# A fused attention, gated-MLP and gated-convolution kernel: its opening issued in another order

## The chip, the cores and the metric

The kernel runs on one core of one Trainium2 chip. The metric is the device time of one execution in microseconds (us). The profile's span, from the first to the last recorded instruction, is a little shorter than that time. The core has five engines that matter here, each with its own in-order instruction queue: TensorE (PE; its weight loads are listed as PEld), VectorE (DVE), ScalarE (ACT), GpSimd (POOL) and SyncE (SP), which here only issues DMA transfers. Semaphores tie the queues together.

## The reference

Three layers in sequence, in float32, on 8 batches of 576 tokens and 512 channels:

```python
scores = scale * q @ k.T                        # per batch and head (8 heads of 64)
x = (scores * Dmat) @ v                         # Dmat: gamma_h ** (i - j) for i >= j, else 0

h = gelu_tanh(x @ w_in)                         # 512 -> 1024
u, v = h[..., :512], h[..., 512:]
v_n = (v - mean(v)) / sqrt(var(v) + 1e-6) * g_ln
v_s = einsum('ts,bsd->btd', w_sg, v_n) + b_sg   # mix over the 576 tokens
x = x + (u * v_s) @ w_out

gate = sigmoid(causal 5-tap convolution of x)
out = (gate * (x @ w_val)) @ w_out2
```

The weights `w_in`, `w_out`, `w_val`, `w_out2` and `conv_w` arrive as float64.

## The kernel before

**Attention** is done in 24 groups (8 batches, three groups of 192 tokens each), and a group in three chunks of 64 tokens. For group i, `load_kq(i)` and `load_v(i)` fetch its keys (384 KB), its queries in three layouts (960 KB) and its values (576 KB) on SP's queue into rings of two buffers. Then come `k_decay` (ACT, four products a chunk), `scores` (PE, 24 products into the PSUM tile `sc`), `masked` (DVE, `sc` times the decay mask into `pt`), `adds` (PE, keys times values into `st`), `states` (DVE, running sums of `st`, a step a chunk), `state_decay` (DVE), `q_decay` (DVE), `outputs` (PE, into `xo`), `out_copy` (ACT, `xo` to `xg`), `out_high` (ACT, the rounded part of x, and the store of x to DRAM on ACT's DMA queue) and `out_low` (DVE, the rest of x). `sc`, `st`, `xo` and `pt` have one buffer each, `sums` and `qp` two. The last group of a batch has two chunks in `adds` and `states`, the first has a smaller `q_decay`. A float32 product of PE leaves two MATMUL and two LDWEIGHTS records in the trace: `scores` 48 of each, `adds` 48 or 32, `outputs` 96, or 80 in the first group of a batch.

**`w_in`** is fetched in four blocks g of 256 columns (1 MB each) into `raw_in`, which has two halves (g % 2), and decoded from float64 bits into a high and a low part, `wi`. `decode` returns ten steps: steps 0 and 9 run on ACT, steps 1, 2, 3, 5 and 7 are DVE tensor_scalar operations, 4, 6 and 8 are DVE scalar_tensor_tensor operations. `d[0]` and `d[1]` are the two parts of block 0, and `d[2]`, `d[3]`, `d[4]` are blocks 1 to 3. All blocks share one set of temporaries, `tmp_in`.

**The MLP's first product** is cut into `u_tile(b, n)` (12 matmuls of 288 columns, blocks 0 and 1 of `w_in`; even n needs tokens 0 to 287, odd n the rest) and `v_tile(b, s)` (12 matmuls of 512 columns, blocks 2 and 3, 128 tokens each; tile 4 of an odd batch holds the last 64 tokens of two batches). `u_gelu`, `v_gelu`, `v_norm` and `v_high` follow on ACT, `v_stat` on DVE and POOL, and `v_low` on DVE. PSUM has two buffers for these tiles. `mix` is the product over tokens; it needs `w_sg` (split by `split_w_sg` on DVE after `fetch_w_sg`, through two `raw` buffers) and all `v` tiles of its batch. The split `w_sg` lies in the buffer that holds x of batch 0, so that `split_w_sg(0)` waits for the last product on that x.

**The order.** From line 721 on, the order of the opening is written out by hand, one call a line, and it is the order within each engine's queue: 49 warm-up products on zeros, `w_in`, the attention groups 0 to 5 and part of 6, and all 16 `u` tiles of batches 0 and 1. From line 926 a planner sorts the rest by due times: the nine `v` tiles of batches 0 and 1 (list `slow`), then `outputs(6)`, the first mix and everything after it.

Of the kernel before, what the change touches and what calls it, by code (L numbers as in the profile page):

```python
# [23 lines left out]
GC = 3  # L24
# [113 lines left out]
def fused_kernel(  # L138
# [50 lines left out]
    with ExitStack() as p1:  # L189
# [268 lines left out]

        def states(i):

            if i >= NGR:
                return
            t = grp[i]
            if i % NG == 0:
                t["sums"] = sts.tile([128, GC, 2, 2 * D], F32, tag="sums", name="sums")
            for j in range(chunks(i)):
                new = t["st"][:, :, 2 * D * j : 2 * D * (j + 1)]
                if j < GC - 1:
                    to = t["sums"][:, j + 1]
# [37 lines left out]

        def out_copy(i):
# [18 lines left out]
        def out_high(i):  # L527
# [17 lines left out]
            act.dma_start(out=x1d[:, i], in_=xc)  # L545
# [83 lines left out]
        def u_tile(b, n):  # L629
            m, h = n // 2, n % 2  # L630
            if n == 0:
                bt[b]["u"] = upool.tile([128, KT, S], F32, tag="u", name="u")
# [101 lines left out]
        sync.dma_start(out=dm_sb, in_=dmask)  # L734
        fetch_w_in(0, 1, 4)
        sync.dma_start(out=kf_sb, in_=kfac)
        load_kq(0)
        load_kq(1)
        d[0][0]()
        sync.dma_start(out=qf_sb, in_=qfac)  # L740
        d[0][1]()
        load_v(1)
        d[0][2]()
        fetch_w_in(1)
        d[0][3]()
        d[0][4]()
        d[0][9]()
        d[0][5]()
        d[0][6]()
        d[0][7]()  # L750
        d[0][8]()
        d[1][0]()
        d[1][1]()
        d[1][2]()
        d[1][3]()
        d[1][4]()
        scores(0, False)
        k_decay(0, act, (0,))
        d[1][5]()
        masked(0)  # L760
        k_decay(0, act, (2,))
        d[1][6]()
        k_decay(0, act, (1,))
        d[1][7]()
        d[1][9]()
        adds(0)
        d[1][8]()
        scores(1, False)
        k_decay(1, act, (1,))
        states(0)  # L770
        k_decay(1, act, (2,))
        k_decay(1, act, (0,))
        q_decay(0)
        state_decay(1)
        outputs(0)
        load_kq(2)
        q_decay(1)
        adds(1)
        out_copy(0)
        masked(1)  # L780
        load_v(2)
        out_high(0)
        states(1)
        load_kq(3)
        d[2][0]()
        d[2][1]()
        outputs(1)
        d[2][2]()
        out_low(0)
        out_copy(1)  # L790
        scores(2, False)
        q_decay(2)
        k_decay(2, act, (1,))
        state_decay(2)
        k_decay(2, act, (0,))
        masked(2)
        out_high(1)
        adds(2)
        d[2][3]()
        load_kq(4)  # L800
        states(2)
        load_v(3)
        out_low(1)
        outputs(2)
        d[2][4]()
        k_decay(3, act, (1,))
        scores(3, False)
        d[2][5]()
        k_decay(3, act, (0,))
        load_v(4)  # L810
        fetch_w_in(2)
        u_tile(0, 0)
        masked(3)
        k_decay(3, act, (2,))
        d[2][6]()
        d[2][9]()
        u_tile(0, 2)
        d[2][7]()
        u_gelu(0, 0)
        d[2][8]()  # L820
        scores(4, False)
        k_decay(4, act, (1,))
        q_decay(4)
        u_tile(0, 4)
        k_decay(4, act, (2,))
        q_decay(3)
        u_gelu(0, 2)
        adds(3)
        out_copy(2)
        u_tile(0, 6)  # L830
        k_decay(4, act, (0,))
        states(3)
        load_kq(5)
        u_gelu(0, 4)
        out_high(2)
        state_decay(4)
        outputs(3)
        u_gelu(0, 6)
        out_low(2)
# [3 lines left out]
        states(4)  # L843
        u_tile(0, 1)
        d[3][0]()
        out_high(3)
        d[3][1]()
        u_tile(0, 5)
        u_gelu(0, 1)
        d[3][2]()  # L850
        out_low(3)
        k_decay(5, act, (0,))
        masked(4)
        u_tile(0, 3)
        u_gelu(0, 5)
        k_decay(5, act, (1,))
        state_decay(5)
        q_decay(5)
        outputs(4)
        u_gelu(0, 3)  # L860
        d[3][3]()
        d[3][4]()
        scores(5, False)
        load_v(6)
        fetch_w_in(3)
        out_copy(4)
        adds(5)
        masked(5)
        out_high(4)
        u_tile(0, 7)  # L870
        d[3][9]()
        out_low(4)
        states(5)
        u_tile(1, 0)
        u_gelu(0, 7)
        d[3][5]()
        d[3][6]()
        outputs(5)
        u_gelu(1, 0)
        d[3][7]()  # L880
        u_tile(1, 2)
        out_copy(5)
        load_v(7)
        d[3][8]()
        load_kq(6)
        out_high(5)
        u_tile(1, 6)
        u_gelu(1, 2)
        out_low(5)
        d[4][0]()  # L890
        u_tile(1, 4)
        u_gelu(1, 6)
        d[4][1]()
        d[4][2]()
        u_tile(1, 1)
        u_gelu(1, 4)
        d[4][3]()
        d[4][4]()
        u_tile(1, 7)
        u_gelu(1, 1)  # L900
        d[4][5]()
        k_decay(6, act, (2,))
        q_decay(6)
        u_tile(1, 5)
        u_gelu(1, 7)
        d[4][6]()
        k_decay(6, act, (0,))
        u_tile(1, 3)
        k_decay(6, act, (1,))
        d[4][7]()  # L910
        d[4][8]()
        u_gelu(1, 5)
        scores(6, False)
        u_gelu(1, 3)
        d[4][9]()
        adds(6)
        masked(6)
        load_kq(8)
        states(6)
        load_kq(7)  # L920
        state_decay(7)
# [3 lines left out]


# [104 lines left out]
        slow = [("v", 0, s) for s in range(4)] + [("v", 1, s) for s in (4, 0, 1, 2, 3)]  # L1031
# [17 lines left out]
        at(0.0, fetch_w_sg, 0)  # L1049
        at(0.0, fetch_w_sg, 1)  # L1050
# [452 lines left out]
```

## Time and profile before

| | us |
|---|---|
| median of 3 executions | 717.16 (717.13 to 718.82) |
| the profiled execution | 717.23 |
| its span | 715.4 |
| PE busy in the span | 692.2 (97%) |
| DVE busy | 567.8 (79%) |
| ACT busy | 387.2 (54%) |
| POOL busy | 137.1 (19%) |

The profiled execution took 1.83 us more than its span, and it lies 0.07 us from the median. PE is idle for 23.2 us of the span. The page cuts the span into 40 slices of 17.9 us; PE's busy tenths there are 3 in the first slice, 7 in the second and in the last, and 9 in the 37 others. So a reader looks at the opening first. A row of the timeline gives start, duration, engine, line, operation, output and inputs and a count. In the chain of work that ended last, a row gives start, length and what the chain passed through; "issue" is time for which the profile shows no releaser.

### The profile page before, as it was taken

To read this page: it belongs to the slowest core of one execution; us is meant where nothing else is said; L and a number is where in the kernel's file an instruction comes from. 1 tells how busy PE (TensorE), PEld (TensorE's weight loads), DVE (VectorE), ACT (ScalarE), POOL (GpSimd) and SP (SyncE) were. 2 spreads that over 40 slices of the span, in tenths; PEclk is the share of its full clock that TensorE was granted. 3 is DMA by queue.
4 is the path that set the end of the run, shared out by engine and by line. 5 is a ranking of instruction groups with operands and counts; after the bars stand their busy time and mean duration, and the time that the engine had idled before them with its cause. 6 is when DMAs were issued, how large, how long until landed. Compare 5 with 4: busy or idle time off the path is not lost.

```text
span 715.4 us, 20119 instructions
## 1 busy us (share of the span) xinstructions
PE 692.2 (97%) x8658; PEld 661.4 (92%) x8658; DVE 567.8 (79%) x899; ACT 387.2 (54%) x692; POOL 137.1 (19%) x210
## 2 busy tenths in 40 slices
PE   3799999999999999999999999999999999999997
PEld 3689889899998998998998999999999999999997
DVE  5677788797697786886865657989899998989893
ACT  5656583562744635536426134676566665656542
POOL 0000340410410302303004002222223231212100
PEclk9689999999999999999999999999999999999999
DMA  9978439699489989498872899899679896745404
GB/s 338 350 273 275 180 105 310 200 289 368 111 242 343 278 252 327 87 304 322 210 226 41 297 393 244 278 223 191 167 166 206 192 213 159 175 118 75 109 1 150
DMA packets 69578, 157.15 MB, mean 220 GB/s; under 512 B 5873, under 2 KB 43889, under 8 KB 67697
## 3 DMA queue, kind: packets, MB, share of 16 engines
q1 hardware_dynamic: 35440, 97.90, 38.9%
q0 software_dynamic: 22016, 39.23, 29.0%
q10 hardware_dynamic: 12032, 18.73, 7.1%
q8 instruction: 68, 1.11, 0.6%
q14 instruction: 22, 0.17, 0.1%
HBM read 109.54 MB, written 54.26 MB: 229 GB/s over the span
## 4 chain that ended last, share of the span: by engine, by line
PE 87%; DVE 5%; DMA 5%; ACT 1%; issue 1%; SPq 1%; DVEq 0%; ACTq 0%
PE ps L1158 24%; PE ps_u L183 14%; PE ps L1277 14%; PE ps_v L568 14%; PE ps_m L655 10%; PE sc L424 3%; DMA raw_g<-g1d 3%; PE xo L502 2%; PE xo L494 2%; DMA qk_sb<-in_qk 2%; PE st L440 2%; PE ps_m L663 2%; DVE op L165 1%; DVE xl L165 1%; ACT op L162 0%
## 5 line engine op out<-in xcount | busy, mean ns | idle before, releaser
L655 PE MATMUL ps_m<-ws,vh 128*128 128x288 f32 x768 | 114.0, 297 | 0.7 <-DVE gt L672 0.7
L655 PEld LDWEIGHTS ps_m<-ws,vh 128*128 128x128 f32 x768 | 104.8, 188 | 2.5 <-DVE gt L672 1.4
L1277 PE MATMUL ps<-op,wv 128*128 128x288 f32 x768 | 102.7, 294 | 0.0
L1277 PEld LDWEIGHTS ps<-op,wv 128*128 128x128 f32 x768 | 101.9, 188 | 0.0
L1158 PE MATMUL ps<-op,wo 128*128 128x288 f32 x672 | 92.2, 297 | 1.1 <-DVE op L165 1.0
L1158 PEld LDWEIGHTS ps<-op,wo 128*128 128x128 f32 x672 | 90.7, 188 | 1.8 <-DVE op L165 1.2
L183 PE MATMUL ps_u<-xh,wi 128*128 128x288 f32 x448 | 91.7, 296 | 0.0
L1158 PE MATMUL ps<-op,wf 128*128 128x288 f32 x672 | 90.8, 296 | 0.0
L1158 PEld LDWEIGHTS ps<-op,wf 128*128 128x128 f32 x672 | 90.1, 188 | 0.0
L1250 DVE SCALAR_TENSOR_TENSOR gate<-x,cw_sb,gate 128x576 f32<-128x576 f32 x114 | 87.5, 812 | 1.0 <-ACT gate L1232 1.0
L183 PEld LDWEIGHTS ps_u<-xh,wi 128*128 128x128 f32 x448 | 72.6, 188 | 0.6
L568 PE MATMUL ps_v<-wi,xh 128*128 128x512 f32 x224 | 70.8, 397 | 0.0
L183 PE MATMUL ps_u<-xl,wi 128*128 128x288 f32 x224 | 66.0, 295 | 0.0
L162 ACT CAST op<-raw_g 128x1152 fp32r<-128x1152 f32 (+1 forms) x36 | 36.7, 1036 | 46.1 <-PE ps L1277 20.5
L514 ACT COPY xg<-xo 128x768 f32<-128x768 f32 x24 | 19.1, 797 | 66.6 <-PE xo L502 60.9
L595 POOL TENSOR_SCALAR rs<-mv 128x1 f32<-128x1 f32 x36 | 10.1, 280 | 229.9 <-DVE mv L594 218.5
L1168 ACT COPY s<-ps 128x576 f32<-128x576 f32 x48 | 30.8, 641 | 37.9 <-PE ps L1158 35.5
L585 ACT ACTIVATE vt<-ps_v 128x512 f32<-128x512 f32 x36 | 21.5, 597 | 53.8 <-PE ps_v L568 53.3
L568 PEld LDWEIGHTS ps_v<-wi,xh 128*128 128x128 f32 x224 | 41.4, 188 | 9.9 <-DVE gt L672 0.2
L672 DVE SCALAR_TENSOR_TENSOR gt<-ps_m,g_sb,b_sb 128x288 f32<-128x288 f32 x64 | 32.8, 515 | 20.9 <-PE ps_m L663 20.8
L1210 POOL DMA_DIRECT2D x<-x1d x24 | 31.3, 1542 | 84.1 <-DVE x L1199 83.2
L165 DVE TENSOR_TENSOR op<-raw_g,op 128x1152 fp32r<-128x1152 f32 (+1 forms) x36 | 42.9, 1202 | 5.5 <-ACT op L162 5.5
(124 smaller groups left out, 1298.3 us busy)
## 6 DMA issues: line engine op xcount, KB each, us to landing
qk_sb<-in_qk SPq DMA_DIRECT2D x24, 960.0 KB, 8.2
raw_g<-g1d SPq DMA_DIRECT2D x8, 2016.0 KB, 8.4
vv_sb<-in_vv SPq DMA_DIRECT2D x24, 576.0 KB, 5.5
g1d<-g1d POOLq DMA_DIRECT2D x48, 288.0 KB, 5.8
g1d<-u SPq DMA_DIRECT2D x40, 288.0 KB, 7.4
kk_sb<-in_kk SPq DMA_DIRECT2D x24, 384.0 KB, 6.0
x1d<-xg ACTq DMA_DIRECT2D x24, 384.0 KB, 6.0
x<-x1d POOLq DMA_DIRECT2D x24, 384.0 KB, 6.8
```

What stands on the lines that cost most here:

```text
L162: return act.copy(dst, src) if engine is act else engine.tensor_copy(dst, src)
L165: return dve.tensor_tensor(dst, src, high.bitcast(F32), op=ALU.subtract)
L183: pe.matmul(ps[:, :n], lhs, rhs[:, k, x_cols], start=i == 0, stop=i == last)
L568: pe.matmul(ps, lhs, rhs, start=i == 0, stop=i == KT * 3 - 1)
L585: act.activation(vt, vs[b, s][0], AF.Gelu_apprx_tanh)
L655: pe.matmul(ps[:, :n], lhs, rhs, start=first, stop=False)
L672: dve.scalar_tensor_tensor(gt, mx.pop((b, i))[:, :n], g_sb[:, m : m + 1], b_sb[:, t0 : t0 + n], op0=ALU.mult, op1=ALU.add)
L1158: pe.matmul(got(ps)[:, o, :HN], lhs, rhs, start=first and i == 0, stop=last and i == 5, skip_group_check=True,)
L1168: add("ACT", act_us(2 * HN), lambda: act.copy(got(key), full(ps)), (ps,), (key,), stage=stage)
L1210: lambda g=g, at=at: pool.dma_start(out=L["x2"][par][:, :, at : at + GT], in_=x1d[:, i * NG + g], accum_op=ALU.add), mine, [("x2", par, "g ...
L1250: lambda gt=gt, x2=x2, m=m, j=j: dve.scalar_tensor_tensor(gt(), x2(j), cw_sb[:, m, j : j + 1], gt(), op0=ALU.mult, op1=ALU.add), (*x2_keys ...
L1277: pe.matmul(ps[:, mm, :HN], lhs, rhs, start=j == 0, stop=j == 3 * KT - 1, skip_group_check=True)
```

## The change

The calls of the opening stand in another order, and more of them stand in it. The nine `v` tiles with all their steps, `q_decay(7)`, `k_decay(7)`, and the fetches and splits of `w_sg` move from the planner's list into the order by hand (`slow` is now empty, and `load_conv` has a due time 25.1 less, as nine tiles of 2.79 are gone from ahead of it). Four helpers are cut finer: `load_kq` into `load_k` and `load_q`, `states` into `state_step`, and the store of x (`out_store`) out of `out_high`. Block 0 of `w_in` is cut into halves (1:1) where it was 1:3. The warm-up products stay. No arithmetic is added or taken away. The first loads, and the middle of the new order:

```diff
-        d = [decode_w_in(0, 0, 1), decode_w_in(0, 1, 4)] + [decode_w_in(g) for g in range(1, 4)]
-        fetch_w_in(0, 0, 1)
+        d = [decode_w_in(0, 0, 2), decode_w_in(0, 2, 4), decode_w_in(1), decode_w_in(2), decode_w_in(3)]
+        fetch_w_sg(1)
+        sync.dma_start(out=dm_sb, in_=dmask)
+        fetch_w_sg(0)
+        load_v(0)
+        load_k(0)
+        sync.dma_start(out=kf_sb, in_=kfac)
+        load_q(0)
+        fetch_w_in(0, 2, 4)
         sync.dma_start(out=gf_sb, in_=gfac)
-        load_v(0)
...
+        load_v(1)
+        load_k(1)
         sync.dma_start(out=qf_sb, in_=qfac)
+        fetch_w_in(0, 0, 2)
+        load_q(1)
         fetch_w_in(1)
...
-        slow = [("v", 0, s) for s in range(4)] + [("v", 1, s) for s in (4, 0, 1, 2, 3)]
+        slow = []
...
-        load_conv(34.0)
+        load_conv(8.9)
```

The order of each queue after the change, up to the first mix (groups and tiles by number; ss is a `state_step`, sd `state_decay`, qd `q_decay`):

```
PE   warm x49, scores 0, adds 0, outputs 0, adds 1, scores 1, adds 2, outputs 1, scores 2, outputs 2,
     u(0,2) u(0,6), scores 3, u(0,4), adds 3, scores 4, u(0,0) u(0,5) u(0,7) u(0,1) u(0,3), outputs 3,
     adds 4, v(0,0) v(0,1), adds 5, scores 5, outputs 4, v(0,2) v(0,3), outputs 5, u(1,4) u(1,0), adds 6,
     u(1,2) u(1,3), v(1,4) v(1,0) v(1,1) v(1,2) v(1,3), u(1,7) u(1,5) u(1,1), scores 6, u(1,6), outputs 6, mix
DVE  d1.3 d1.5, masked 0, d1.6, ss 0.0, d1.1, ss 0.1, d1.2, qd 0, ss 0.2, d1.4 d0.3 d1.7 d0.5 d1.8 d0.1,
     sd 1, d0.2, ss 1.0, qd 1, out_low 0, d0.4 d0.6 d0.7, ss 1.1, d0.8, ss 1.2, d2.3, sd 2, masked 1, qd 2,
     d2.1, ss 2.0, d2.2, ss 2.1, d2.4 d2.5 d2.7, masked 2, d2.6, out_low 1, d3.1 d2.8 d3.2 d3.5 d3.3 d3.6 d3.4,
     masked 3, d3.7, out_low 2, d3.8 d4.1, ss 3.0, d4.5 d4.3 d4.6 d4.2, qd 3, d4.4, ss 3.1, d4.7, ss 3.2, d4.8, ...
SP   w_sg 1, dmask, w_sg 0, v 0, k 0, kfac, q 0, w_in 0 (half), gfac, v 1, k 1, qfac, w_in 0 (half), q 1,
     w_in 1, k 2, q 2, v 2, k 3, w_in 2, q 3, k 4, v 3, q 4, w_in 3, v 4, k 5, q 5, v 5, k 6, q 6, ...
```

In the kernel before, PE ran all 16 `u` tiles before the first `v` tile, and the first `u` tile stood after `scores(3)`.

## Rows read from the trace of the kernel before

**Rows 1.** Windows: length; busy us (records) of each engine; PEclk; DMA share; GB/s.

```profile
10.00:20.00 10.00, 5.67 (x211) 5.27 (x215) 8.68 (x14) 6.10 (x24) 0.00 (x0) 0.95 1.01 414
20.00:30.00 10.00, 6.93 (x256) 6.42 (x250) 6.32 (x10) 6.71 (x16) 0.00 (x0) 0.67 0.94 339
30.00:40.00 10.00, 8.40 (x164) 7.72 (x157) 7.69 (x11) 5.09 (x14) 0.00 (x0) 0.53 0.96 358
```

**Rows 2.** The chain that ended last, of 0 to 160: start, length, what.

```profile
26.52 1.91 issue
...
36.41 4.75 PE ps_u L183 x24
41.16 0.86 PE sc L424 x48
...
54.64 0.28 PE xo L494 x8
...
62.30 11.35 PE ps_u L183 x84
...
75.22 25.34 PE ps_v L568 x108
100.57 0.39 PE xo L502 x16
...
101.89 1.78 PE ps_m L655 x12
```

**Rows 3.** DVE by line and shape, 0 to 110: busy, mean ns of one, idle.

```profile
L474 DVE TENSOR_TENSOR sums<-st,sums 128x256 f32<-128x256 f32 x19 | 8.0, 423 | 3.0 <-PE st L440 2.5
L452 DVE TENSOR_TENSOR pt<-sc,dm_sb 128x768 f32<-128x768 f32 x8 | 7.6, 955 | 6.2 <-PE sc L424 5.4 <-PE xo L502 0.8
L236 DVE SCALAR_TENSOR_TENSOR wi<-tmp_in 128x1024 fp32r<-128x1024 f32 x3 | 3.7, 1225 | 0.1
L235 DVE TENSOR_SCALAR tmp_in<-tmp_in 128x1024 uint32<-128x1024 uint32 x3 | 2.1, 687 | 0.0
L236 DVE SCALAR_TENSOR_TENSOR wi<-tmp_in 128x768 fp32r<-128x768 f32 x1 | 1.0, 959 | 0.0
```

**Rows 4.** DVE timeline: two neighbours on other data, then two on the same.

```profile
51.15 0.95 DVE L165 TENSOR_TENSOR xl<-xg,xh 128x768 fp32r<-128x768 f32 x1
52.02 0.95 DVE L452 TENSOR_TENSOR pt<-sc,dm_sb 128x768 f32<-128x768 f32 x1
...
61.49 0.69 DVE L235 TENSOR_SCALAR tmp_in<-tmp_in 128x1024 uint32<-128x1024 uint32 x1
62.21 1.23 DVE L236 SCALAR_TENSOR_TENSOR wi<-tmp_in 128x1024 fp32r<-128x1024 f32 x1
```

**Rows 5.** SP timeline: issue of q 0 and of w_in 2.

```profile
4.25 0.63 SPq L380 DMA_DIRECT2D qk_sb<-in_qk  x1
...
35.56 0.42 SPq L253 DMA_DIRECT2D raw_in<-in_w_in  x1
```

**Rows 6.** DMA issues alone: q 0, w_in 2, w_in 1: KB, us to landing.

```profile
qk_sb<-in_qk SPq DMA_DIRECT2D x1, 960.0 KB, 7.5
...
raw_in<-in_w_in SPq DMA_DIRECT2D x1, 1024.0 KB, 7.4
...
raw_in<-in_w_in SPq DMA_DIRECT2D x1, 1024.0 KB, 12.7
```

**Rows 7.** PE timeline: the part of scores 1 ahead of PE's first halt.

```profile
15.25 0.78 PE L424 MATMUL sc<-qk_sb 64*64 64x64 f32 x28 [0.48 <-DMA qk_sb<-in_qk]
```

**Rows 8.** PE alone, from the end of one halt to the next (clock, DMA).

```profile
22.40:28.42 6.02, 3.90 (x127) 0.72 0.94 326
28.42:33.79 5.37, 3.77 (x127) 0.57 0.94 341
```

**Rows 9.** Windows of 2 us around the first u tiles, columns as in rows 1.

```profile
36.00:38.00 2.00, 2.00 (x22) 1.88 (x17) 1.53 (x2) 0.01 (x1) 0.00 (x0) 0.50 0.94 330
...
40.00:42.00 2.00, 2.00 (x58) 1.77 (x56) 1.89 (x3) 2.00 (x10) 0.00 (x0) 1.00 0.62 254
```

More of the change, by code (lines that the diff above doesn't have):

```diff
@@ L764, in fused_kernel @@
+        state_step(0, 0)
+        k_decay(1, act, (0,))
+        d[1][1]()
+        state_step(0, 1)
+        d[1][2]()
+        k_decay(1, act, (2,))
+        q_decay(0)
+        state_step(0, 2)
+        outputs(0)
+        load_q(2)
+        k_decay(1, act, (1,))
+        d[1][4]()
+        d[0][3]()
+        d[1][9]()
         d[1][7]()
-        d[1][9]()
-        adds(0)
+        d[0][5]()
+        d[0][0]()
         d[1][8]()
-        scores(1, False)
-        k_decay(1, act, (1,))
-        states(0)
@@ L771, in fused_kernel @@
[L771 to L777, printed above, removed]
         adds(1)
         out_copy(0)
-        masked(1)
[L781 to L785, printed above, removed]
+        load_v(2)
+        d[0][1]()
+        state_decay(1)
+        load_k(3)
+        scores(1, False)
+        out_store(0)
+        out_high(0, False)
+        d[0][2]()
+        state_step(1, 0)
@@ L786, in fused_kernel @@
+        q_decay(1)
+        out_low(0)
+        d[0][4]()
+        d[0][6]()
+        d[0][9]()
+        d[0][7]()
+        k_decay(2, act, (0,))
+        fetch_w_in(2)
+        state_step(1, 1)
+        d[0][8]()
+        d[2][0]()
+        state_step(1, 2)
+        d[2][3]()
+        k_decay(2, act, (1,))
+        load_q(3)
+        state_decay(2)
+        masked(1)
+        q_decay(2)
+        adds(2)
         d[2][1]()
         outputs(1)
+        k_decay(3, act, (1,))
+        load_k(4)
+        state_step(2, 0)
@@ L811, in fused_kernel @@
[L811 to L821, printed above, removed]
-        k_decay(4, act, (1,))
[L823 to L828, printed above, removed]
+        k_decay(3, act, (0,))
+        state_step(2, 1)
+        d[2][4]()
+        k_decay(3, act, (2,))
@@ L842, in fused_kernel @@
         load_v(5)
[L843 to L850, printed above, removed]
-        out_low(3)
[L852 to L856, printed above, removed]
-        state_decay(5)
[L858 to L862, printed above, removed]
-        scores(5, False)
[L864 to L921, printed above, removed]
+        masked(4)
+        v_tile(0, 0)
+        load_k(6)
+        out_high(3, False)
+        state_step(4, 0)
+        q_decay(4)
+        out_store(3)
+        out_low(3)
+        load_q(6)
+        state_step(4, 1)
+        v_tile(0, 1)
+        q_decay(5)
+        v_gelu(0, 0)
+        state_step(4, 2)
+        v_stat(0, 0)
+        state_decay(5)
+        k_decay(6, act, (0,))
+        adds(5)
+        v_gelu(0, 1)
+        scores(5, False)
+        state_step(5, 0)
         sync.dma_start(out=b_sb, in_=b_sg)
@@ L924, in fused_kernel @@
         sync.dma_start(out=conv_raw.rearrange("p n t -> p (n t)"), in_=conv_w)
+        load_k(7)
+        k_decay(6, act, (2,))
+        v_stat(0, 1)
+        outputs(4)
+        load_q(7)
+        state_step(5, 1)
+        k_decay(6, act, (1,))
+        v_tile(0, 2)
+        masked(5)
+        load_v(6)
+        v_norm(0, 0)
+        v_norm(0, 1)
+        q_decay(6)
+        v_high(0, 0)
+        v_high(0, 1)
+        v_low(0, 0)
+        out_copy(4)
+        v_low(0, 1)
+        v_tile(0, 3)
@@ new lines, in fused_kernel @@
+        v_gelu(0, 2)
+        k_decay(7, dve)
+        out_high(4, False)
+        v_stat(0, 2)
+        out_store(4)
+        out_low(4)
+        outputs(5)
+        v_gelu(0, 3)
+        split_w_sg(0)
+        v_norm(0, 2)
+        v_stat(0, 3)
+        u_tile(1, 4)
+        fetch_w_sg(2)
+        v_high(0, 2)
+        split_w_sg(1)
+        load_v(7)
+        out_copy(5)
+        v_low(0, 2)
+        out_store(5)
+        out_high(5, False)
+        u_tile(1, 0)
+        fetch_w_sg(3)
+        q_decay(7)
@@ new lines, in fused_kernel @@
+        v_norm(0, 3)
+        out_low(5)
+        adds(6)
+        u_gelu(1, 4)
+        v_high(0, 3)
+        u_tile(1, 2)
+        split_w_sg(2)
+        u_gelu(1, 0)
+        load_k(8)
+        state_step(6, 0)
+        fetch_w_sg(4)
+        u_tile(1, 3)
+        v_low(0, 3)
+        u_gelu(1, 2)
+        state_step(6, 1)
+        state_step(6, 2)
+        state_decay(7)
+        v_tile(1, 4)
+        u_gelu(1, 3)
+        split_w_sg(3)
+        split_w_sg(4)
+        v_tile(1, 0)
+        v_gelu(1, 4)
```

218 lines of the change are left out of this document (141 added, 77 removed).

## The prediction

> **What bounds the kernel now.** I read the slices of the page first: PE is the bound (97% busy), and nearly all of its idle time lies in the first two slices and the last. Then the windows of the opening [rows 1]: between 10 and 40 us PE is busy for 5.67, 6.93 and 8.40 of each 10 us, its granted clock falls to 0.67 and 0.53, the DMA engines are at 0.94 to 1.01 of their time, and DVE at 6.3 to 8.7. Last the chain of waits [rows 2]: from the first u tile at 36.41 to the first mix at 101.89 it is PE nearly throughout. So the change, which adds and removes no arithmetic, moves the total by as much as it moves the start of the first mix; behind that the queues are the same, PE has no idle time to win, and no transfer that the change delays is still under way. I predict that start.
>
> PE's work from the first v tile on is fixed in the new order: nine v tiles, 25.34; eight u tiles at 11.35 / 7 = 1.62, 12.97; outputs 4 and 5 as from 54.64 to 56.19, 1.55 each; outputs 6, from 100.57 to 101.89, 1.32; scores 5 and 6 at 0.86 and at 0.70 (the stretch before 56.89 is of that kind; I take 0.8 each); adds 5 and 6, with two thirds and all of the products of a scores, 0.5 and 0.75 [rows 2]. Sum 45.6 us. **The start of the first v tile** therefore decides: before, it stood at 75.22 with all 16 u tiles done; now only eight u tiles stand ahead of it, so it must come by 101.89 - 45.6 = 56.3 us for a draw.
>
> **The change part by part. Loads.** q 0 was issued at 4.25 and landed after 7.5, at 11.75 us [rows 5, 6]; 3080 KB had been asked for on SP's queue by then. Block 2 of w_in landed at 35.56 + 7.4 = 42.96 with 13960 KB asked for on SP and ACT. That is 349 KB a us, in the order of issue. The new order puts 576 KB of w_sg, needed only at 70 us, ahead of everything. By the same line the first half block of w_in (3142 KB) lands at 12.0 us, q 1 (5960 KB) at 20.0, block 1 (6984) at 23.0, q 2 (8328) at 26.8, v 2 (9288, with one store of x) at 29.6, block 3 (14984, with two stores) at 45.9. In the kernel before DVE had decoded since 5.3 us; now its first step waits until 12.0.
>
> **DVE** must finish step d4.8 before the first v tile. Its queue up to there: three blocks of five steps of 0.687 and three of 1.225, 7.11 each, 21.3; block 0 in halves, 7.11 plus eight extra starts (1225 ns for 1024 columns and 959 for 768 leave 0.16 at no columns), 8.4; masked x4 at 0.955, 3.8; state_step x11 at 0.423, 4.65; q_decay x4 as masked, two of them of two thirds the size, 3.2; out_low x3 as masked and one small as a state_step, 3.3; state_decay x2, 0.85 [rows 3]. Sum 45.5. Neighbours that don't depend on each other start 0.87 apart where one takes 0.95 (92%), dependent ones 0.72 where one takes 0.69 (104%) [rows 4]. The new order mixes unrelated steps, so I take 95%, 43.2, between ends of 41.9 and 45.5. With no wait DVE is done at 12.0 + 43.2 = 55.2. One wait I can see: `state_step(2,0)` stands 18.5 us of work down the queue, at 12.0 + 17.6 = 29.6, and needs adds 2, which needs v 2 (29.6) and takes 1.0 at the low clock. That is 1.0 more: 56.2.
>
> **PE up to the first v tile.** adds 2 stands ahead of outputs 1 in PE's queue, so outputs 1, scores 2 and outputs 2 all wait for v 2. From 30.6: outputs 1, 96 records, to 33.3 (127 such records kept PE busy for 3.77 us at a clock of 0.57 [rows 8], 0.0297 each with short waits in it; I take 0.028); scores 2 to 34.7; outputs 2, behind masked 2, which by DVE's queue ends near 35.7, to 38.4. `out_low(1)` is done at 12.0 + 0.95 x 25.8 + 1.0 = 37.5, before that. So u(0,2) starts at 38.4 or later, against 36.41 for the first u tile before.
>
> Here a cost has to be added that no dependence names: PE halted several times with no releaser in the profile, once for 1.91 us inside scores 2 [rows 2]. The first halt came after 28 of the 48 MATMUL records of scores 1 [rows 7], which is record 222 (98 of warm-up, 48 of scores 0, 48 of adds 0). Later, from the end of one halt to the next, PE ran 127 MATMUL records and as many weight loads, in 6.02 and 5.37 us [rows 8]; I read each as a block of instructions. Counted on from 222, the ends of blocks fall at 28 of 80 records of outputs 0, 27 of 48 of scores 1, 74 of 96 of outputs 1 and 57 of 96 of outputs 2 in the new order. The first three stand where PE waits anyway. The last could not be passed before 32.7 + 5.4 = 38.1 (6.0: 38.7), with 39 records, 1.1 us, still to come: 39.2 to 39.8. The cost is 0 to 1.4; I take 0.4, because the 6.02 and 5.37 were met with DMA at 0.94 [rows 8] and SP's new queue asks for nothing between 25 and 30.6. So u(0,2) at 38.8.
>
> [...]
>
> From 38.8: eight u tiles 12.97; scores 3, 4 and adds 3 at 0.86, 2.6; outputs 3 and adds 4, 1.32 and 0.75 [rows 2]. [...] Sum 18.6: **v(0,0) at 57.4**, just behind DVE's 56.2. The first mix starts at 57.4 + 45.6 = 103.0, 1.1 later than at 101.89.
>
> **The other moved steps** cost nothing. The splits of w_sg (five pairs) and the v steps run under 45.6 us of unbroken PE work, in which DVE and ACT have as much room as before; `split_w_sg(0)` waits for v(0,3), as it did. SP's queue holds its loads behind `fetch_w_in(2)`, which waits for the low words of block 0 (d0.6, near 24.5); q 3 and k 4 behind it land by 38, before scores 3 and k_decay 4 want them. adds 5 needs v 5, issued after outputs 3 near 55 and landed 60, wanted at 62. If one of these is late by a us, PE stands for that us.
>
> **Rivals.** (1) *The values of group 2 hold the whole opening.* Every queue is in order, and adds 2 is the neck: DVE's `state_step(2,0)`, PE's outputs 1 and 2 and all u tiles are behind it. v 2 is issued near 19.0; if it takes not 10.6 but 12.7, as block 1 of w_in did [rows 6], it lands 2.1 later and all behind it comes 2.1 later: mix at 105.1, total 720.4. With the halt and the clock at their dear ends too, 721.7. From 1.0 us of extra lateness on, this makes the kernel measurably slower. For it: the 576 KB in front, and DMA full until 40. Against it: block 2 took 7.4 with DMA as full [rows 1, 6], and 10.6 is in the sum already. (2) *Both queues pack.* DVE at 92% without a wait is done at 53.9; PE with the clock up and no halt ends outputs 2 at 36.5 and 17.6 later, at 54.1, is ready for v(0,0). Mix at 99.8, total 715.1. For it: DVE was idle for 7.3 of the 30 us from 10 to 40 before [rows 1], which the new order could close. Against it: DVE's floor of 41.9 behind a half block that can't land long before 12.0; so a gain beyond 2.3 us has no room. (3) *The change does not do what it says*: the same neck, other names; that is nearly the forecast.
>
> **How the numbers follow.** The profiled execution is 717.23 us, its span 715.4, 0.07 from the median of 717.16. Forecast: 717.23 + 1.1 = 718.3 us, no difference that a measurement can tell from none, which is about 0.3% or 2.15 us (715.0 to 719.3); its own range, with the halt from 0 to 1.4, the clock from 0 to 1.5 and DVE's spacing, is 716.2 to 720.0; chance 0.55. Rival 1, 720.4 (up to 721.7): 0.27. Rival 2, 715.1 (down to 714.8): 0.18. The range takes both in: 714.8 to 721.7. Of the forecast's 0.55, 0.42 lies within 0.3%, 0.11 above and 0.02 below; rival 1 is slower; of rival 2, 0.10 is faster and 0.08 the same. So faster 0.12, the same 0.50, slower 0.38.
>
> **What the profile after would show.** Right: the first u tile at 38 to 40, DVE nearly full from 12 to 56 us, v(0,0) at 56 to 59, the first mix at 102 to 104, and PE full behind it. If v(0,0) starts by 54 with DVE dense, rival 2 holds; if adds 2 starts after 31.5 and outputs 1 behind it, rival 1. Wrong altogether would be idle PE time after the first mix, a v tile waiting for its buffer, or DVE starting well before 12 us.

## The result, and the profile after

The changed kernel takes **725.6 us** (median of 4 runs, 724.9 to 726.4) where the kernel before takes 718.0 beside it (717.1 to 719.4): a ratio of 1.0104, interval 1.0080 to 1.0128. It is slower, by 7.6 us where 1.1 was forecast, and the time lies outside the range, on the side of rival 1. The profiled execution is 725.0, its span 723.2 against 715.4: 7.8.

In the experiments' groups single runs of one kernel, the kernel before included, scatter by up to 12 us, so steps are read from the profiles there and totals are given as ratios with their intervals.

| start, us | before | forecast | after |
|---|---|---|---|
| first u tile (chain) | 36.41 | 38.8 | 40.97 |
| first v tile (chain) | 75.22, all u done | 57.4 | 60.31 |
| first mix (chain) | 101.89 | 103.0 | 110.37 |
| span | 715.4 | | 723.2 |

The first mix is 8.48 us later, the span 7.8 longer: the loss is made in the opening, as the forecast assumed, and nothing is given back or lost behind it (715.4 - 101.89 = 613.5, 723.2 - 110.37 = 612.8).

The windows of the opening, columns as in [rows 1]:

```profile
20.00:30.00 10.00, 3.18 (x100) 2.81 (x95) 9.75 (x19) 5.57 (x13) 0.00 (x0) 1.00 1.02 416
30.00:40.00 10.00, 7.28 (x245) 6.93 (x248) 6.37 (x9) 6.93 (x19) 0.00 (x0) 1.00 0.71 241
80.00:90.00 10.00, 7.46 (x85) 6.63 (x77) 8.36 (x15) 4.91 (x10) 1.43 (x2) 1.00 0.55 190
```

Between 20 and 30 us PE is busy for 3.18 where it was 6.93 before, DVE for 9.75 where it was 6.32 [rows 1]. From 30 on DVE has gaps (6.37), and PE has a gap again at 80 to 90 us, where the forecast had it full. The chain, columns as in [rows 2]:

```profile
20.16 9.68 DMA vv_sb<-in_vv
...
30.09 1.13 PE st L448 x32
...
33.31 1.78 issue
...
40.97 4.98 PE ps_u L183 x24
...
60.31 5.78 PE ps_v L585 x24
...
110.37 1.78 PE ps_m L672 x12
```

PE's timeline of the same kernel shows the waits themselves: start, length, what, and in brackets the idle time ahead and its releaser.

```profile
24.41 0.91 PE L432 MATMUL sc<-qk_sb 64*64 64x64 f32 x21 [2.13 <-issue]
30.09 1.13 PE L448 MATMUL st<-vv_sb,kk_sb 64*64 64x64 f32 x32 [4.78 <-DMA vv_sb<-in_vv]
...
35.09 0.38 PE L512 MATMUL xo<-pt,vv_sb 64*64 64x64 f32 x3 [1.78 <-issue]
...
38.34 0.49 PE L512 MATMUL xo<-pt,vv_sb 64*64 64x64 f32 x8 [0.85 <-DVE pt L460]
...
83.18 0.40 PE L183 MATMUL ps_u<-xh,wi 128*128 128x288 f32 x1 [2.54 <-ACT u L658]
...
104.55 0.40 PE L183 MATMUL ps_u<-xh,wi 128*128 128x288 f32 x1 [0.72 <-ACT u L658]
```

**Loss 1, ahead of the first u tile.** PE waits 4.78 us for v 2, as forecast (landed at 20.16 + 9.68 = 29.84; forecast 29.6). Then it halts 1.78 inside outputs 1, after 74 of 96 records, with no releaser: one of the ends of blocks that the forecast had counted. The halt of 2.13 inside scores 1 is another; it stands ahead of the wait for v 2 and costs nothing. Masked 2, behind scores 2 on DVE, adds 0.85.

**Loss 2, behind the first v tile.** PE stands 2.54 and 0.72 us for a copy of an earlier u tile out of PSUM on ACT. ACT's timeline says why it came late:

```profile
78.42 0.81 ACT L619 ACTIVATE vt<-vt,rs 128x512 f32<-128x512 f32 x1 [2.98 <-POOL rs L614]
...
82.02 0.81 ACT L619 ACTIVATE vt<-vt,rs 128x512 f32<-128x512 f32 x1
82.74 0.39 ACT L658 ACTIVATE u<-ps_u 128x288 f32<-128x288 f32 x1
```

`u_gelu(1, 4)` (L658) stands in ACT's queue behind `v_norm(0, 2)`, `out_copy(5)`, `out_high(5)` and `v_norm(0, 3)` (L619 are the norms). The first norm waited 2.98 us for the statistics of its rows, which go through DVE and three small steps on POOL. From its start to that of the u copy lie 4.3 us more of ACT's work (78.42 to 82.74), with one gap of 0.40. The pool of PSUM that the u tiles write has two buffers, and both were full; so PE waited for ACT, and ACT had waited for POOL and then had other work ahead of the copy. The second wait, of 0.72, is of the same kind: `u_gelu(1, 7)` stands behind `v_norm(1, 2)`, which waited 1.45 us for POOL.

DVE's timeline answers the forecast's sum for that engine:

```profile
13.89 0.43 DVE L228 TENSOR_SCALAR tmp_in<-raw_in 128x512 uint32<-128x512 uint32 x1 [12.89 <-DMA raw_in<-in_w_in]
...
37.33 0.96 DVE L460 TENSOR_TENSOR pt<-sc,dm_sb 128x768 f32<-128x768 f32 x1 [2.35 <-PE sc L432]
...
57.57 1.22 DVE L236 SCALAR_TENSOR_TENSOR wi<-tmp_in 128x1024 fp32r<-128x1024 f32 x1
```

It began at 13.89 (forecast 12.0), ended d4.8 at 58.8 (56.2), and so was ready ahead of PE's 60.31, as forecast.

### The profile page after: what moved, and what is told of

Read it like the earlier page. It is cut to its first block, busy times and chain, and to the rows that moved or that the text cites. A ratio compares the mean times of both kernels' runs of the same rounds, so it can differ in the third digit from the quotient of the medians.

```text
span 723.2 us, 20119 instructions
## 1 busy us (share of the span) xinstructions
PE 693.5 (96%) x8658; PEld 662.3 (92%) x8658; DVE 565.3 (78%) x899; ACT 386.1 (53%) x692; POOL 138.5 (19%) x210
## 3 DMA queue, kind: packets, MB, share of 16 engines
q8 instruction: 68, 1.11, 0.6%
## 4 chain that ended last, share of the span: by engine, by line
PE 87%; DMA 4%; DVE 4%; ACT 2%; issue 1%; SPq 1%; POOL 1%; ACTq 0%; POOLq 0%; DVEq 0%
PE ps L1258 24%; PE ps_u L183 14%; PE ps L1377 14%; PE ps_m L672 12%; PE ps_v L585 12%; PE xo L512 3%; DMA vv_sb<-in_vv 2%; PE xo L504 2%; PE sc L432 2%; PE ps_m L680 2%; PE st L448 2%; DMA w7d<-raw 1%; ACT vt L619 1%; DVE pt L460 1%; POOL rs L613 0%
## 5 line engine op out<-in xcount | busy, mean ns | idle before, releaser
L689 DVE SCALAR_TENSOR_TENSOR gt<-ps_m,g_sb,b_sb 128x288 f32<-128x288 f32 x64 | 32.8, 515 | 25.6 <-PE ps_m L680 25.4
L412 ACT ACTIVATE kk_sb<-kk_sb,kf_sb 128x64 f32<-128x64 f32 x184 | 46.9, 335 | 7.2 <-DMA kk_sb<-in_kk 7.2
```

What stands on the lines that cost most here:

```text
L412: act.mul(k[:, j, n], k[:, j, n], kf_sb[:, j, n : n + 1])
L689: dve.scalar_tensor_tensor(gt, mx.pop((b, i))[:, :n], g_sb[:, m : m + 1], b_sb[:, t0 : t0 + n], op0=ALU.mult, op1=ALU.add)
```

## Experiments

Three suspects stand for the loss: w_sg in front of all loads; adds 2 ahead of outputs 1, with the halt behind it; and the u copies behind the v norms on ACT. Each was undone alone first. In a timeline the changed kernel's first u tile, first v tile and first mix stand at 40.90, 60.24 and 110.30, 0.07 ahead of the chain; differences below are between rows of one kind.

A profile is one execution, and openings scatter too. The kernel with the u copies moved has the same calls as the changed kernel up to the first v tile, and the edit of the last kernel below leaves the order of every queue as it was. Their first u tiles start at 40.24 and 39.80 in the chain (40.97 in the changed kernel), their first v tiles at 58.50 and 58.52 in the timeline (60.24); the last kernel's first mix comes at 108.02 (110.30). So a step of 1.2 us at the first u tile, of 1.8 at the first v tile or of 2.3 at the first mix can't be told from scatter by one profile.

**w_sg behind load v 6.**

```
-        fetch_w_sg(1)
         sync.dma_start(out=dm_sb, in_=dmask)
-        fetch_w_sg(0)
...
         load_v(6)
+        fetch_w_sg(1)
+        fetch_w_sg(0)
```

> The changed kernel with the two w_sg fetches (576 KB) moved from the front of SP's queue to behind the load of v 6. Theory (the loads' order feeds the neck at adds 2): at 349 KB a us everything behind them lands 1.6 us earlier, v 2 near 28.2 instead of 29.84, the first u tile starts near 39.3 instead of 40.97, total 1.6 us less than the changed kernel's 725.6, so 724. Rival (what holds the opening is PE's halt inside outputs 1, not the load): v 2 lands earlier, but the halt still ends near 35 and the first u tile stays within 0.5 us of 40.97; total 725.6.

Ratio 1.0142 (1.0082 to 1.0202), 4 runs. PE's timeline:

```profile
9.18 1.56 PE L432 MATMUL sc<-qk_sb 64*64 64x64 f32 x48 [5.09 <-DMA qk_sb<-in_qk]
...
33.24 0.28 PE L512 MATMUL xo<-pt,vv_sb 64*64 64x64 f32 x3 [2.61 <-issue]
...
81.78 0.43 PE L183 MATMUL ps_u<-xh,wi 128*128 128x288 f32 x1 [3.92 <-ACT u L658]
...
110.44 1.84 PE L672 MATMUL ps_m<-ws,vh 128*128 128x288 f32 x12
```

The window of the two u tiles behind that wait, columns as in [rows 1]:

```profile
81.78:86.76 4.98, 4.98 (x25) 4.98 (x26) 4.14 (x10) 1.18 (x3) 0.00 (x0) 0.66 0.53 183
```

Scores 0 start 3.2 us earlier (12.35 in the changed kernel), the first u tile 2.65 (38.25), the first v tile 3.0 (57.25). But the first mix starts at 110.44, no earlier at all, and the total is no lower. PE's wait for the u copy grew from 2.54 to 3.92, since `split_w_sg` on DVE waited 1.27 for the load that now came late and the statistics of the second norm stood behind it. After that wait the two u tiles ran at a mean granted clock of 0.66 and took 4.98 us where they took 3.45 in the changed kernel. The two, 1.4 and 1.5, are what had been won. What the loads cost is real; here it was lost again at loss 2, the longer wait being in part this edit's own doing.

**adds 2 behind outputs 1.**

```
-        adds(2)
         d[2][1]()
         outputs(1)
+        adds(2)
```

> The changed kernel with adds 2 behind outputs 1 in PE's queue, so that outputs 1 and its part of the chain no longer wait for v 2. Theory A (the next block of instructions is on its way as soon as PE enters a block, at 24.4 us): outputs 1 starts near 28.3, no halt in it, scores 2 near 32, first u tile near 39.5, total 1.5 us less than 725.6. Theory B (the next block is asked for only once PE runs on in the block, so the time PE stands waiting does not count): outputs 1 starts near 28.3 and halts until about 33.2, adds 2 comes after that near 34, DVE's state_step(2,0) waits 3 us longer, first u tile near 41.5, total 0.5 us more.

Ratio 1.0074 (1.0044 to 1.0105), from 8 of 9 runs. PE's timeline:

```profile
28.86 0.49 PE L512 MATMUL xo<-pt,vv_sb 64*64 64x64 f32 x8 [2.90 <-DVE pt L460]
...
31.26 1.08 PE L448 MATMUL st<-vv_sb,kk_sb 64*64 64x64 f32 x32
...
39.57 5.13 PE L183 MATMUL ps_u<-x_sb,wi 128*128 128x288 f32 x24
...
108.86 1.85 PE L672 MATMUL ps_m<-ws,vh 128*128 128x288 f32 x12
```

The halt inside outputs 1 is gone, as theory A said; the block now ends 10 records into adds 2, and PE runs through it. The first u tile comes 1.3 us earlier than in the changed kernel and the first mix 1.4. That is no more than the scatter above (scores 0 start 0.4 later here, and the first v tile, at 58.99, comes no earlier than in the kernel below, at 58.50), and the interval of the ratio overlaps the changed kernel's: what this order alone is worth is not shown.

**u copies further ahead in ACT's queue.**

```
         u_tile(1, 4)
+        u_gelu(1, 4)
...
         v_gelu(1, 3)
+        u_gelu(1, 7)
         v_norm(1, 2)
```

(with both taken from their later places)

> The changed kernel with u_gelu(1,4) and u_gelu(1,7) each moved ahead of a v_norm in ACT's queue, next to their u tiles. Theory (PE's idle time behind the first v tile is a full pair of PSUM buffers, because the copy out of u(1,4) stands on ACT behind v_norms that wait for POOL): the two idle stretches at 80.4 to 83.2 and 103.6 to 104.6 close, the first mix starts 3.3 us earlier than 110.37, total 722.3. Rival (ACT is late as a whole, or the v tiles' chain over POOL holds PE anyway): PE waits a few tiles later instead, less than 1 us gained, total above 724.6.

Ratio 1.0062 (1.0029 to 1.0094), 10 runs. PE's timeline:

```profile
82.06 0.40 PE L183 MATMUL ps_u<-xh,wi 128*128 128x288 f32 x1 [1.60 <-ACT u L658]
...
106.61 1.84 PE L672 MATMUL ps_m<-ws,vh 128*128 128x288 f32 x12
```

ACT's timeline, and from the chain the first two u tiles, which lie ahead of the edit:

```profile
76.44 0.82 ACT L619 ACTIVATE vt<-vt,rs 128x512 f32<-128x512 f32 x1 [2.96 <-POOL rs L614]
77.16 0.39 ACT L658 ACTIVATE u<-ps_u 128x288 f32<-128x288 f32 x1
```

```profile
40.24 3.96 PE ps_u L183 x24
```

From the first v tile (58.50) to the first mix it takes 48.11 us, 1.95 less than the 50.06 of the changed kernel and 1.4 less than the 49.50 of the last kernel below; PE's idle time there fell from 3.26 to 1.60, the rest being `u_gelu(1, 0)`, which still stood behind `out_copy(5)`, `out_high(5)` and `v_norm(0, 3)`. The other 1.7 us by which the mix comes earlier arose ahead of the edit and are no effect of it. `u_gelu(1, 4)` still stands behind `v_norm(0, 2)`, and that norm still waited 2.96 us for POOL. What the edit took from ahead of this copy is the work between the norms and the second norm; so for the wait of 2.54 the order of ACT's own work is shown as a cause, and the share of the wait for POOL was not tried alone. `u_gelu(1, 7)` did move ahead of the norm that waits for POOL, and its 0.72 is gone.

**37 warm-up products, and 57.** `WARM` counts PE's products on zeros at the start; one is two MATMUL records.

```
-WARM = 49
+WARM = 37
```

> The changed kernel with 37 warm-up products instead of 49, 24 MATMUL records fewer ahead of everything. Theory (PE halts at the ends of blocks of 127 MATMUL records, wherever they fall): the halt after 27 records of scores 1 and that after 74 of 96 records of outputs 1 vanish; ends of blocks now fall 24 records later in the program, after 52 of outputs 0, 3 of adds 2, 2 of scores 2 and 81 of outputs 2, and a halt shows at the start of scores 2, until about 35. Rival (the halts belong to these operations, a buffer or a wait that the profile doesn't show): they stay where they were, at 27 of scores 1 and 74 of outputs 1. Total within 1.5 us of 725.6 by either.

```profile
34.77 0.86 PE L432 MATMUL sc<-qk_sb 64*64 64x64 f32 x43 [1.79 <-issue]
...
39.48 0.38 PE L504 MATMUL xo<-qp,sums 64*64 64x64 f32 x4 [1.40 <-issue]
```

With 24 records less, each end of a block should come 24 records later in the program. It does: none is left inside scores 1 or outputs 1, one stands after 2 records of scores 2 and one after 81 of outputs 2. A third, of 1.45 us, stands inside adds 4, ahead of the first v tile. So the halts go by the count of PE's instructions, and belong to no operation. One run of 729.77 (kernel before beside it: 718.5): the ends moved in the whole program, and from the first mix to the end it takes 619.6 us, with three halts of 3.6 us in all inside later scores. In the ten profiles here with 49 warm-up products that stretch takes 612 to 617, with no halt over 0.6 us in it. The total is therefore no measure of the opening.

```
-WARM = 49
+WARM = 57
```

> The changed kernel with 57 warm-up products, 16 MATMUL records more ahead, so ends of blocks fall 16 records earlier: after 11 of 48 records of scores 1 and after 58 of 96 of outputs 1. When PE then stands before adds 2 it has run 37 records into its block, not 21. Theory P (the next block is asked for at a fixed place some 22 to 29 records into a block, and comes 4 to 6 us after PE has passed it): it comes while PE waits for v 2, and outputs 1 has no halt; the first u tile starts 1 to 1.8 us earlier than at 40.9. Theory A (asked for as the block is entered, but slow while DMA is full) and theory B (time in which PE waits never counts): outputs 1 halts after 58 records until about 35, as before, the first u tile stays near 40.9. The total is no measure here, since the ends of blocks move in the whole program.

```profile
22.02 1.33 PE L432 MATMUL sc<-qk_sb 64*64 64x64 f32 x37 [0.23 <-issue]
...
35.20 0.38 PE L512 MATMUL xo<-pt,vv_sb 64*64 64x64 f32 x3 [2.97 <-issue]
```

The ends moved 16 records ahead, as they should (scores 1 is cut after 11 records, outputs 1 after 58). I had expected that a block of which 37 records had run before the wait for v 2 would bring the next one in time. It did not: PE halted for 2.97. Behind the first mix this kernel, too, took longer, 618.3 us, with two halts of 3.0 us in all.

**The three together**: w_sg behind load q 6, adds 2 behind outputs 1, `u_gelu(1, 4)` and `(1, 0)` right behind their tiles, `u_gelu(1, 7)` ahead of the norm.

```
-        fetch_w_sg(1)
         sync.dma_start(out=dm_sb, in_=dmask)
-        fetch_w_sg(0)
...
-        adds(2)
         d[2][1]()
         outputs(1)
+        adds(2)
...
+        fetch_w_sg(1)
+        fetch_w_sg(0)
         sync.dma_start(out=b_sb, in_=b_sg)
...
         u_tile(1, 4)
+        u_gelu(1, 4)
...
         u_tile(1, 0)
+        u_gelu(1, 0)
...
+        u_gelu(1, 7)
         v_norm(1, 2)
```

> The changed kernel with all three repairs: the two w_sg fetches behind the load of q 6, adds 2 behind outputs 1, and u_gelu(1,4), u_gelu(1,0) and u_gelu(1,7) ahead of the v_norms. Theory (three losses in a row on PE's path: loads and adds 2 ahead of the first u tile, about 4 us; copies behind v_norm on ACT, 3 to 4): first u tile near 37, first mix near 102 to 103, total within 1.5 us of the kernel before. Rival (DVE's decoding, which starts late, sets the first v tile whatever PE does): the first v tile stays near 58, DVE is full up to it, and the first mix comes no earlier than 105, total 3 us or more above the kernel before.

Ratio 1.0029 (1.0004 to 1.0054), 12 runs. PE's timeline, then two windows:

```profile
36.77 4.24 PE L183 MATMUL ps_u<-x_sb,wi 128*128 128x288 f32 x24
...
102.69 1.85 PE L672 MATMUL ps_m<-ws,vh 128*128 128x288 f32 x12
```

```profile
30.00:40.00 10.00, 6.94 (x162) 6.50 (x155) 10.00 (x14) 9.33 (x23) 0.00 (x0) 0.74 0.94 334
40.00:50.00 10.00, 10.00 (x200) 9.54 (x199) 10.00 (x15) 6.27 (x15) 0.00 (x0) 1.00 0.53 198
```

The first mix comes at 102.69, 7.6 of the 8.5 us earlier (5.3 by the 108.02 of the last kernel below), outside the scatter, and about 0.75% of the 1.04% is won back: the three suspects together are most of the loss. The total was expected within 1.5 us of the kernel before; 0.29% is 2.1. Now DVE is full from 30 to 50 us (10.00 of 10), and the kernel still does not beat the one before.

**The kernel before with only w_sg in front.**

```
+        fetch_w_sg(0)
+        fetch_w_sg(1)
         fetch_w_in(0, 0, 1)
...
-        at(0.0, fetch_w_sg, 0)
-        at(0.0, fetch_w_sg, 1)
```

> The kernel before with only the two w_sg fetches (576 KB) moved to the front of SP's queue. Theory (what stands ahead in SP's queue comes off the start of everything): q 0 lands 1.6 to 3 us later than at 11.75, the first u tile starts 1.6 to 3 us later than at 36.4 and the total is 1.6 to 3 us more than the kernel before. Rival (the kernel before has slack at its loads, its first u tile waits for PE's halts and DVE): the first u tile moves less than 0.7 us and the total is the same.

Ratio 1.0113 (1.0061 to 1.0164), 4 runs. PE's timeline:

```profile
14.81 1.56 PE L424 MATMUL sc<-qk_sb 64*64 64x64 f32 x48 [10.72 <-DMA qk_sb<-in_qk]
...
38.65 3.96 PE L183 MATMUL ps_u<-x_sb,wi 128*128 128x288 f32 x24
...
103.84 1.85 PE L655 MATMUL ps_m<-ws,vh 128*128 128x288 f32 x12
```

In the other kernel the same 576 KB cost 2.9 us at scores 0 (11.93 before), 2.3 at the first u tile and 2.0 at the first mix. The total lost more than that: its interval starts at 0.61%, 4.4 us, above the 1.6 to 3 expected. In the profile the stretch behind the first mix took 616.9 us where it took 613.5 before; why was not followed up.

**Decoding ahead of the first masks**: in the kernel with the three edits, the second half of block 0 of w_in was loaded first and decoded before masked 0, to start DVE early.

```
+        fetch_w_in(0, 2, 4)
         sync.dma_start(out=dm_sb, in_=dmask)
...
+        d[1][0]()
+        for x in (3, 1, 2, 4, 5, 6, 7, 8):
+            d[1][x]()
         k_decay(0, act, (0,))
```

(with the same steps taken from their later places)

> The kernel with the three repairs (e5_three), and the half block of w_in as the first load, decoded on DVE ahead of masked 0. Theory (what is left of the loss is DVE's late start: it was idle until about 11 us and full from 30 to 58): DVE starts near 5, its queue behind masked 0 is 3.9 us shorter, q 0 lands 1.5 us later; the first v tile starts near 53 instead of 55.3, the first mix near 100.5, total some 1.5 us below the kernel before. Rival (q 0 is on the path of everything, so what is put ahead of it costs as much as DVE gains): the first v tile stays at 55 to 56.5, total at or above e5_three's.

Ratio 1.0040 (1.0013 to 1.0066), 12 runs. PE's timeline:

```profile
11.44 1.56 PE L432 MATMUL sc<-qk_sb 64*64 64x64 f32 x48 [7.36 <-DMA qk_sb<-in_qk]
...
23.95 0.80 PE L432 MATMUL sc<-qk_sb 64*64 64x64 f32 x19 [3.29 <-issue]
...
56.55 5.85 PE L585 MATMUL ps_v<-wi,x_sb 128*128 128x512 f32 x24
```

The first v tile comes at 56.55, 1.25 later than at 55.30 with the three edits alone. DVE started at 5.39 and still ended d4.8 at 55.47 (54.18 with the three edits): scores 0 started 1.6 later behind the larger load, PE halted 1.44 inside outputs 0 and 3.29 inside scores 1 (1.85 there with the three edits), and DVE stood still for 3.00 us until adds 2. So DVE's lead can't be bought in this way; what it would be worth without these costs is not shown.

**When does a block of instructions come?** The page's list of DMA queues has one whose count fits PE's instructions:

```profile
q8 instruction: 68, 1.11, 0.6%
```

68 packets of 1.11 MB / 68 = 16.3 KB, for 2 x 8658 = 17316 matmuls and weight loads: 254.6 of them a packet, the 127 pairs between two halts [rows 8]. So I read every block as one packet, and the trace has its time. In the changed kernel one goes out at 21.88 and PE resumes at 24.41; one at 32.67 and PE resumes at 35.09. In the 29 halts of the first 62 us of all twelve kernels, the one before included, PE resumes 2.2 to 2.6 us after the packet. That time is the same for a halt of 0.96 us (2.5, the kernel before, at 22.4) as for one of 2.13 (2.5, the changed kernel, at 24.41): what differs is when the packet goes out. Two theories remain, and q 2 put behind v 2 tells them apart, since it releases adds 2 sooner with the same bytes in line.

```
-        load_q(2)
...
         load_v(2)
+        load_q(2)
```

> The changed kernel with q 2 asked for right behind v 2 instead of ahead of it, so that adds 2 is released about 2.5 us sooner (27.3 to 27.8 instead of 30.09); the same bytes lie on the queue until about 33. In the trace of the changed kernel one 16 KB packet of PE's instruction queue (queue 8) goes out at 32.67, and PE comes out of its halt inside outputs 1 2.4 us later, at 35.09; in four other runs of this order the packet goes out 2.2 to 3.3 us after adds 2 is released. Theory R: PE asks for the block late, some time after the waiting adds 2 is released; then the packet goes out at 29.5 to 31, the halt ends at 32 to 33.5, and outputs 1 ends about 2 us sooner. Theory L: the request stands in line behind the loads that were asked for before it, and goes out when that line has drained; then the packet stays at 31.8 to 33, PE halts for 3 to 5 us and comes out of it at 34.3 to 35.5 as before, and nothing is gained by an earlier v 2.

```profile
26.86 1.62 PE L448 MATMUL st<-vv_sb,kk_sb 64*64 64x64 f32 x29 [2.11 <-DVE sums L479]
...
32.95 0.38 PE L512 MATMUL xo<-pt,vv_sb 64*64 64x64 f32 x3 [2.27 <-issue]
...
38.76 3.71 PE L183 MATMUL ps_u<-x_sb,wi 128*128 128x288 f32 x24
...
107.92 1.84 PE L672 MATMUL ps_m<-ws,vh 128*128 128x288 f32 x12
```

adds 2 was released 3.2 us sooner, the packet went out at 30.37, 2.3 sooner, with the DMA engines at 0.97 to 1.04 of their time up to 33 us, and the halt ended at 32.95. In this run theory R holds and theory L falls. One run took 722.57 beside 715.94 of the kernel before.

```
-        fetch_w_in(2)
...
-        load_q(3)
...
         outputs(1)
+        fetch_w_in(2)
+        load_q(3)
```

> The changed kernel with block 2 of w_in and q 3 (1984 KB, asked for at 24.9 and 25.4 us) asked for behind outputs 1 only, so that the line of loads drains at about 30 instead of 33; adds 2 is released at 30 as before. Theory R (PE asks for the next block of instructions only some us after adds 2 is released): the packet of PE's instruction queue goes out at 32 to 33 and the halt inside outputs 1 stays at 1.5 to 2.6 us. Theory L (the request waits in line behind the loads): the packet goes out as soon as v 2 and k 3 have landed, at 29 to 31, PE has the block by 33.5, and the halt inside outputs 1 shrinks to 0.3 us or nothing. Under both the decoding of block 2 comes later, which may cost some us behind the first v tile; only the opening is read here.

```profile
28.67 1.13 PE L448 MATMUL st<-vv_sb,kk_sb 64*64 64x64 f32 x32 [4.62 <-DVE qp L418]
...
34.49 0.28 PE L512 MATMUL xo<-pt,vv_sb 64*64 64x64 f32 x3 [2.60 <-issue]
```

This edit did not do what it was meant to: SP waits for none of PE's outputs there, so both loads were still asked for at 24.43 and 24.85, and the line stayed full until 33. It says nothing on a short line. It is one more halt of the same kind: packet at 32.08, 3.4 us after adds 2 was released; one run, 724.91.

In all seven kernels with adds 2 ahead of outputs 1 the packet went out 2.2 to 3.5 us after adds 2 was released (at 26.9 to 30.1 us), and PE halted for 1.5 to 3.0. With adds 2 behind outputs 1, PE stood still for DVE's masked 1 instead, 1.8 to 3.2 us. There the packet went out 1.3 us (adds 2 alone) and 0.6 us (three edits) before PE was released, with no halt; with the decoding ahead it went out 0.9 us after, and PE halted for 0.4. What makes PE ask stays open: a count of records run does not do it (37 run before the wait were not enough with 57 warm-up products, 29 were with adds 2 behind), and waiting alone does not forbid it. Over the whole program no packet of the changed kernel goes out more than 136 MATMUL records ahead of its own block, by the count from record 222 (the packets at 47.65 and 53.56 us); a block is 127.

## Why the prediction was wrong

The forecast set the first mix at 103.0; it came at 110.37, 7.4 us later. Of that some 2 us are scatter between executions: with the order of every queue the same, it came at 108.09 (chain) in the last kernel above. The numbers below are those of the changed kernel's own profile. One more window of the changed kernel, from the first v tile to the first mix, columns as in [rows 1], is needed for the steps behind the first v tile:

```profile
60.31:110.37 50.06, 46.80 (x653) 40.01 (x653) 32.63 (x60) 27.45 (x55) 14.21 (x27) 1.00 0.46 160
```

By the forecast's own steps:

- **"The first three [block ends] stand where PE waits anyway": wrong for the third, +2.2 at the first u tile.** The records were counted right: the halt stands after 74 of 96 of outputs 1, to the record. But a block end hides under a wait only if the next block comes during that wait, and the forecast assumed that it does. It came after the wait: 32.67, 2.6 us behind the release of adds 2. The halt of 1.78 is most of the 40.97 - 38.8; adds 2 began 0.5 later than forecast (30.09 for 29.6). The last end, for which I had taken 0.4, cost nothing: its packet went out at 36.28. The row that should have warned me is [rows 8]: PE ran 127 records and stood still between two halts, so a block was never early there.
- **The clock term, 1.0 in the sum of 18.6: +0.7 in this execution, and scatter.** The work in that sum is 17.6; the other 1.0 was my estimate for a low clock at the first u tiles, and no run shows it. Before the change the first two u tiles took 4.75 us where 24 records of a later stretch take 3.24 [rows 2], 1.5 more, with the granted clock at 0.50 from 36 to 38 us and at 1.00 from 40 to 42 [rows 9]. In the changed kernel they took 4.98. That is 1.74 more, above the upper end of 1.5, and the granted clock reads 1.00 there (window 40.97 to 45.95). But with the u copies moved, and the same calls up to here, they took 3.96, 0.72 more than 3.24, behind a halt of 1.51 and the same wait of 0.85 for masked 2. So the 0.7 is a difference between executions, and no step that failed.
- **"DVE and ACT have as much room as before": wrong, +3.3 behind the first v tile.** ACT had the room: it was busy for 27.45 of 50.06 us there, PE for 46.80. What failed was its order. The new order puts u copies behind norms that wait for POOL and behind other work of ACT, and more u tiles in a row than their PSUM pool has buffers. I had weighed room (busy shares) and not the line: which instruction stands ahead of the one that PE waits for, and on whom that one waits. The forecast named the cover ("45.6 us of unbroken PE work") but looked for late DMA, not for a late copy.
- **The sum 45.6, +1.2.** PE was busy for 46.80 us in that window. By the chain that is nine v tiles 25.6 (25.34 taken), eight u tiles 13.9 (12.97), outputs 4.3 (4.42), scores 1.6 (1.6), adds 1.5 (1.25). The u tile was mis-sized: 1.62 comes from 84 records back to back [rows 2], and here a tile of 12 among other work takes 1.78 on the chain. With the three suspects undone the stretch took 47.39, of which 0.4 is idle.
- **Right:** v 2 as the neck (29.84 for 29.6, with some luck: it was issued at 20.16 for 19.0 and took 9.68 for 10.6, two errors that cancel), DVE done just before PE needs it (58.8 against 60.31), the mechanism of rival 1 at its place, and that nothing behind the first mix gives or takes. Rival 1 had its price wrong (v 2 was not late; the price came from the halt behind it), so its 721.7 was no bound. By its own terms, 718.3 + 2.1 + 1.0 + 0.5, that end is 721.9; and the lower end of the forecast's own range, 716.2, is 716.9 by its terms (0.4 and 1.0 less). Neither slip changes the account.
- **w_sg in front: inside the forecast, but undersized.** I took 1.6 us by bytes (576 KB at 349 KB a us). Both kernels show more: 3.2 at scores 0 when it is taken away from the new, 2.9 when it is added to the old. With scatter, scores 0 start at 11.5 to 12.8 in the seven profiles of the new order with w_sg in front, and at 9.2 and 9.8 in two without it. It did not show as an error: v 2 landed as forecast, and DVE's late start (13.89 for 12.0) was hidden behind PE's neck.

The halts stood in the trace before the change [rows 7, 8], and the page of the kernel before has the same 68 packets on q8. In the changed kernel's first 36 us PE halted for 2.13 and 1.78 us at ends of blocks, where the forecast had counted the ends and had taken 0.4 us for all of them.

The mechanism was thus half right. Taking w_sg away moved the first u tile, moving the u copies shortened the stretch behind the first v tile, and adds 2 behind outputs 1 took the halt away, with a gain that one profile can't show. The three together brought the first mix to 102.69 and the ratio to 1.0029. That is near the forecast's 103.0 and 718.3 / 717.2 = 1.0015, and it was reached only with the two things undone that I had costed at nothing and w_sg out of the way.

## What to carry to other kernels

An engine with time to spare can still stop PE (ACT, busy for 27.45 of 50.06 us, held it for 2.54 and 0.72): for every PSUM buffer that PE reuses, read which instructions stand ahead of the freeing copy in its queue and what they wait for; put copies that free PSUM ahead of work that PE does not wait for, and above all ahead of steps that wait for a long chain of statistics (with `u_gelu(1, 7)` ahead of its norm the 0.72 was gone). A stall may hide under another only if what it waits for can come during that other; otherwise they add up (4.78 for v 2 and 1.78 behind it). Before an edit is credited with a step, compare profiles of kernels that are the same up to that step. And the count of PE's instructions was part of the schedule here: 8 warm-up products more and 12 fewer moved the block ends that were read by 16 and 24 records, and halts of 3.0 and 3.6 us in all stood behind the first mix, far from the edit, in one profile each.

## What the hardware showed unexpectedly

- The page of the changed kernel has 68 packets of 16.3 KB on q8, one for 254.6 of PE's matmuls and weight loads; PE, where it halts in the openings, resumes 2.2 to 2.6 us after a packet goes out. Behind the wait for v 2 the packet went out 2.2 to 3.5 us after the release, with 21 records of the block run before the wait (changed kernel) as with 37 (57 warm-up products).
- The granted clock in the profile of the changed kernel reads 1.00 in every slice, though its first 24 u products took 4.98 us instead of 3.24. So the reading does not go with the pace there, and what slowed these products in that execution is not shown. In the run with adds 2 behind outputs 1, where the same products took 5.06, the record reads 0.50 from 38 to 42 us.
- In the profile of the changed kernel a step of one element in each of 128 rows on POOL took 0.57 us, and 0.98 to 1.13 beside some work of DVE:

```profile
76.92 1.10 POOL L613 TENSOR_TENSOR rs<-rs,nh_sb 128x1 f32<-128x1 f32 x1
...
91.54 0.57 POOL L613 TENSOR_TENSOR rs<-rs,nh_sb 128x1 f32<-128x1 f32 x1
```

In that trace up to 380 us, the 8 of 31 such steps that took 0.98 to 1.13 all lay for 0.55 to 0.70 us beside a DVE TENSOR_TENSOR of L165 or L405; three that lay beside L165 for at most 0.45 took 0.57. Beside masked (L460) for 0.38 to 0.57 us, or the statistics (L610) alone for 0.36 to 0.57, they took 0.57 too, as beside an idle DVE; so in this trace a busy DVE alone does not go with the longer time. This was only read from the timeline, not tried, and no cause is shown.
